# Oldest of four PSUM banks for the small products of attention, and a new order at both ends of it

## Chip, cores and metric

One core of one Trainium2 chip runs the whole program. The metric is device time in microseconds (us), the median over runs of the kernel. PE is TensorE, PEld its weight loads, DVE VectorE, ACT ScalarE, POOL GpSimd, SP SyncE, whose queue issues nearly all DMAs.

## The reference, cut to what matters

```python
scores = scale * q @ k^T                       # 4 batches, 12 heads, 448 x 448, head size 64
scores = einsum('bhij,hg->bgij', scores, w_pre)    # heads are mixed
attn   = softmax(scores)
attn   = einsum('bhij,hg->bgij', attn, w_post)     # heads are mixed again
x      = attn @ v                              # as 1792 tokens x 768
h      = x @ w_in                              # 768 x 2048
x      = (h - tanh(h)) @ w_out                 # 2048 x 768
# then a soft mixture of 8 experts with 4 slots each (phi, w1, w2), output 1792 x 768
```

## The kernel before

Attention (`talking_heads`) cuts each batch's 448 queries into four chunks (120, 120, 120, 88), 16 chunks in all. A chunk is cut into slots of up to 10 queries times 12 heads = 120 rows; there are 180 slots. A slot is the unit of the steady loop: `regroup` (DMA D<-S, issued four slots ahead), `premix` (PE pm, DVE row maximum mx), `expo` (ACT e), `guard`, `recip`, `norm` (POOL and DVE, giving wk), and three slots later `postmix` (PE tm, ACT aT).

Beside these, the loop carries work that prepares or ends whole chunks:

- heads: the scores of a chunk (`scores4`, three calls of two head pairs each), six matmuls sc for each pair and two PSUM banks; ACT copies them to S, the two copies of the odd pair in the slot of the call and those of the even pair in the next slot. S has two buffers, so the copies of chunk m wait until the D<-S of chunk m-2 have read theirs.
- jobs: `k_pair` (transposes kx of the next batch's k, read by ACT as khi and by DVE as klo), `q_half` (transposes qx, read by ACT and DVE as qT), `values` (32 matmuls vx, read by DVE as xs; the third group of a chunk also stores xs to xd). The DVE read of a job stands in the next slot, behind that slot's reciprocal.

The order is written by hand. `plan` puts each piece into a slot before the loop is emitted. Heads stand at fixed slots; `calm` puts q and value jobs into the slot of a window with the least planned PE load. Each engine and the SP queue run in program order.

The PSUM tiles of attention go round eight banks. Two are the premix's (tag p), two the postmix's (t), two have the tag x and two the tag q. Before, kx, vx, qx (from chunk 1 on) and the odd pairs' sc share the two x banks; the even pairs' sc and the first chunk's qx have the two q banks. The q banks' pool closes four slots before the end, when the second part (`moe_and_slots`) starts beside attention's last slots: it splits x and w_in into high and low parts (`split_x`, `split_w`), runs its first two products (hp) and their gates between the last slots, and enters its own loop over 64 products (`step`) when attention has ended (`box["go"]`). Weights go round a ring of three units: `load_w(t)` fills one, `split_w(t)` splits it (ACT, then DVE or POOL), `save_w(t)` stores the split.

From the second part's loop the program goes on to the experts, whose weights are loaded into buffers as the loop frees them.

Of the kernel before, what the change touches and what calls it, by code (L numbers as in the profile page):

```python
# [9 lines left out]
FP32 = mybir.dt.float32  # L10
F32R = mybir.dt.float32r
ACTF = mybir.ActivationFunctionType
# [6 lines left out]
NR = 4  # L19
# [21 lines left out]
def bits(ap):  # L41
    return ap.bitcast(FP32)
# [104 lines left out]
def talking_heads(tc, ident, q, k, v, w_pre, w_post, xd, box, follow):  # L147
# [7 lines left out]
    DB = 5  # L155
    T_LAG = 3
    WARM = 10

    late_stack = ExitStack()
    early_stack = ExitStack()  # L160
# [36 lines left out]
    def kron(name, w, scale, inner_g):  # L197
# [15 lines left out]
            out=m, in_=m, pattern=neg, compare_op=ALU.is_ge, fill=0.0, base=NH - 1, channel_multiplier=-1)  # L213
        return m

    def k_pair(b, p):
        x = ps.tile([128, NR, JP], FP32, tag="x", name="kx", bufs=2)
        src = nat_k.pop((b, p))
        for r in range(NR):
            if b:  # L220
                nc.tensor.transpose(
                    out=x[:, r, :], in_=src[:, r].rearrange("p e d -> p (e d)"), identity=ident[:JP, :JP])
            else:
                for e in range(2):
                    nc.tensor.matmul(
                        x[64 * e:64 * e + 64, r, :], lhsT=src[:, e, r, :], rhs=ident[:JP, :JP], start=True, stop=True)
        x = x.rearrange("p r j -> p (r j)")
        hi = er.tile([128, SEQ], F32R, tag=f"khi{p}", name="khi", bufs=1)
        lo = er.tile([128, SEQ], F32R, tag=f"klo{p}", name="klo", bufs=1)
        nc.scalar.activation(out=hi, in_=x, func=ACTF.Copy)  # L230
        kT[b, p] = hi, lo

        def rest():
            nc.vector.tensor_tensor(out=lo, in0=x, in1=bits(hi), op=ALU.subtract)  # L234

        return rest

    def q_half(n, hf):
        ni = chunks[n][2]
        if hf == 0:  # L240
            qT[n] = er.tile([128, 2, NP, CHUNK], F32R, tag="qT", name="qT")
        t = qT[n][:, :, 3 * hf:3 * hf + 3, :ni]
        x = ps.tile([128, 3, CHUNK], FP32, tag="x", name="qx", bufs=2) if n else psq.tile(
            [128, 3, CHUNK], FP32, tag="q", name="qx")
        for i in range(3):
            p = 3 * hf + i
            nc.tensor.transpose(out=x[:, i, :ni], in_=nat_q[n][:ni, 2 * p:2 * p + 2, :], identity=ident[:ni, :ni])  # L247
        nc.scalar.activation(out=t[:, 0], in_=x[:, :, :ni], func=ACTF.Copy)

        def rest():  # L250
            nc.vector.tensor_tensor(out=t[:, 1], in0=x[:, :, :ni], in1=bits(t[:, 0]), op=ALU.subtract)  # L251

        return rest

    def scores(n, p, on_dve=False):
        b, i0, ni, _ = chunks[n]
        if n not in S_t:
            S_t[n] = er.tile([CHUNK, NH, SEQ], FP32, tag="S", name="S")
        if p % 2:
            xs = [ps.tile([CHUNK, SEQ], FP32, tag="x" if n else "p", name="sc", bufs=2) for _ in range(2)]  # L260
        else:
            xs = [psq.tile([CHUNK, SEQ], FP32, tag="q", name="sc") for _ in range(2)]
        hi, lo = kT[b, p]
        for i, (kt, l) in enumerate(((hi, 0), (lo, 0), (hi, 1))):
            for e in range(2):
                s = slice(64 * e, 64 * e + 64)
                nc.tensor.matmul(  # L267
                    xs[e][:ni], lhsT=qT[n][s, l, p, :ni], rhs=kt[s], start=(i == 0), stop=(i == 2))

        def keep(e):  # L270
            dst = S_t[n][:ni, 2 * p + e, :]
            if on_dve and e:
                nc.vector.tensor_copy(out=dst, in_=xs[e][:ni])
            else:
                nc.scalar.activation(out=dst, in_=xs[e][:ni], func=ACTF.Copy)  # L275

        return [lambda: keep(0), lambda: keep(1)]

# [61 lines left out]
    def values(n, g):  # L340
        b, i0, ni, _ = chunks[n]
        a = attn_t[n]
        if g == 0:
            xs_t[n] = lt.tile([128, NP, CHUNK], FP32, tag="xs", name="xs", bufs=1)
        xs = xs_t[n]
        x = ps.tile([128, 2, CHUNK], FP32, tag="x", name="vx", bufs=2)
        for i in range(2):
            for c in range(NR):
                for e in range(2):
                    h = 4 * g + 2 * i + e  # L350
                    nc.tensor.matmul(  # L351
                        x[64 * e:64 * e + 64, i, :ni], lhsT=nat_v[b, h // NP][:, h % NP, c, :], rhs=a[:, c, h, :ni],
                        start=(c == 0), stop=(c == NR - 1))

        def rest():
            nc.vector.tensor_copy(out=xs[:, 2 * g:2 * g + 2, :ni], in_=x[:, :, :ni])
            if g == 2:
                nc.sync.dma_start(out=xd[b][:, :, i0:i0 + ni], in_=xs[:, :, :ni])

        return rest  # L360
# [4 lines left out]
    def plan(kind, s, *a):  # L365
        at.setdefault((kind, s), []).append(a)
# [12 lines left out]
    for m in range(1, NC):  # L379
        w = len(chunks[m - 1][3])  # L380
        w0 = start[m - 1] - D_AHEAD
        for g in range(3):
            s0 = max(-1, w0 + g * w // 3)
            plan("head", s0, m, g)
            if s0 >= 0:
                load["pe"][s0] += 1.6
            for t in (s0, s0 + 1):
                load["act"][max(t, 0)] += 1.08
    for m in range(1, NC):
        if chunks[m][1] + CHUNK >= SEQ and m + 1 < NC:  # L390
            w = len(chunks[m - 1][3])
            w0 = start[m - 1] - D_AHEAD
            free_at = {}
            for p in range(NP):
                t = w0 + p // 2 * w // 3 + 1 + p % 2
                free_at[p] = t
                job(t, k_pair, chunks[m + 1][0], p, act=0.55, dve=0.62, pe=0.5)
                plan("load", max(t - 6, free_at.get(p - 4, 0) + 1), load_k, chunks[m + 1][0], p)
    for m in range(2, NC):
        t0 = start[m - 2]  # L400
        plan("load", max(0, t0 - 8), load_q, m)
        for lo, hi, hf in ((max(2, t0 - D_AHEAD + 1), t0 + 3, 0), (t0 + 4, start[m - 1] - D_AHEAD - 1, 1)):
            job(calm("pe", lo, hi), q_half, m, hf, act=0.47, dve=0.53, pe=0.4)
    for m in range(NC):
# [42 lines left out]
        nc.tensor.matmul(warm, lhsT=ident, rhs=ident, start=True, stop=True)  # L447
    for p in range(NP):
        k_pair(0, p)()
        if p in (0, 2):  # L450
            q_half(0, p // 2)()
        if p == 3:
            load_q(1)
        if p >= 2:
            for f in scores(0, p - 2, True):
                f()
    for p in range(NP - 2, NP):
        for f in scores(0, p, True):
            f()
    for s in range(D_AHEAD):  # L460
        regroup(s)
    q_half(1, 0)()
# [8 lines left out]
    s = 0  # L471
    while s < NS + T_LAG + 2 or jobs or late:
        live = s < NS
        if s + D_AHEAD < NS:
            regroup(s + D_AHEAD)
        for f, *a in at.get(("load", s), []):
            f(*a)
        if live:
            premix(s)
        if 0 <= s - 1 < NS:  # L480
            recip(s - 1)
        if 0 <= s - 1 < NS:
            norm(s - 1)
        for f in late:
            f()
        late = []
        if 0 <= s - T_LAG < NS:
            postmix(s - T_LAG)
        if live:
            expo(s)  # L490
            guard(s)
        for a in at.get(("head", s), []):
            halves += scores4(*a)
        for f in halves[:2]:
            f()
        halves = halves[2:]
        for f, *a in at.get(("dve", s), []):
            f(*a)
        for f, *a in at.get(("act", s), []):
            f(*a)  # L500
        jobs += at.get(("job", s), [])
        room = 2
        while jobs and room > 0:
            f, *a = jobs.pop(0)
            late.append(f(*a))
            room -= 1
        for f in box["setup"][s - 6:s - 5] if s >= 6 else []:
            f()
        if s == NS - D_AHEAD:
            early_stack.close()  # L510
            more = follow()
        if more is not None:
            next(more)
        s += 1
# [8 lines left out]
def moe_and_slots(tc, ident, xd, wi, wo, wo4, wis, consts, w1, w2, out, box):  # L523
# [107 lines left out]
    def load_w(t):  # L631
        if t < NF:
            nc.sync.dma_start(out=unit(t)[:, :, 1], in_=wi[t].rearrange("p (m i) -> p m i", m=2))
        elif t < NST:
            nc.sync.dma_start(out=unit(t), in_=wis[t % NF])
# [230 lines left out]
    def step(t):  # L866
# [4 lines left out]
            hooks.setdefault(c, []).append(lambda: fn(*a))  # L871

        if t + 2 < LAST + 2:
            load_w(t + 2)
        else:
            on(KD // 2, load_half, t + 2, 0)
            on(KD, load_half, t + 2, 1)
# [74 lines left out]
    gate_last(0)  # L952
    save_w(0)
    load_w(3)
    split_w(2, nc.vector)
    save_w(1)
    yield
    gate_act(1)
    gate_first(1)
    gate_last(1)  # L960
    while not box.get("go"):
        yield
    acc_stack = ExitStack()
    acc = acc_stack.enter_context(tc.tile_pool(name="m_acc", bufs=1, space=PSUM, reuse_waits="tile"))
    for tag in ("h2", "q0", "q1", "r0", "r1", "lg"):
# [310 lines left out]
```

## Time and profile before

| | us |
|---|---|
| median of three runs | 990.23 |
| lowest, highest | 986.09, 991.73 |
| the profiled execution: time | 987.97 |
| the profiled execution: span from first to last instruction | 986.3 |
| span: PE busy | 924.7 |
| span: ACT busy, DVE busy | 571.6, 563.0 |

Busy time of an engine is the time in which it has work in hand; matmuls are pipelined, so a busy PE isn't PE at its peak. Idle time before an instruction is put down to what released it. The granted clock of TensorE is 1.00 at 2.4 GHz; 1.2 GHz stands as 0.5, and a window over both has a value between. In the trace's time the slots run from 23.45 us (first pm) to about 506 us (last pm), and the second part's loop starts at 527.39 us.

### The profile page before, as it was taken

Reading aid. Unit: us, or ns where it says so; the run is one execution under the profiler, and the core shown is the slowest. Engines: PE = TensorE matmul, PEld = TensorE weight load, DVE = VectorE, ACT = ScalarE, POOL = GpSimd, SP = SyncE. Lnnn points to the kernel's source line nnn. Section 1 sums busy time; section 2 is a strip of 40 time slices with the busy share of each in tenths; the row PEclk is TensorE's granted clock in tenths of the full one; section 3 lists DMA queues with packets and bytes.
Section 4 is the critical chain, followed back from the end, with each engine's and each line's share of the span. In section 5 each row is a group of like instructions: output and inputs, shape, how many; then the busy total and the mean of one; then the engine's idle time right before and its main releaser. Section 6 shows DMA issues by size and latency. Waiting matters only on the chain.

```text
span 986.3 us, 19398 instructions
## 1 busy us (share of the span) xinstructions
PE 924.7 (94%) x6952; PEld 685.0 (69%) x6952; DVE 563.0 (57%) x1251; ACT 571.6 (58%) x1291; POOL 267.7 (27%) x467
## 2 busy tenths in 40 slices
PE   8899999989999899999997999999999999789975
PEld 6576777767777677777786777778868877535532
DVE  3476566666566565676544566667677766620103
ACT  4677666766677566777664676547647645401013
POOL 1365445544456344565531222000000000000000
PEclk9999999999999899999998999999999999969988
DMA  4888467885678755685347877688455457689998
GB/s 114 229 217 229 159 204 211 226 233 174 185 211 222 215 179 171 190 254 193 136 164 256 312 260 280 252 348 310 161 194 179 145 143 271 263 316 416 422 396 295
DMA packets 139634, 230.22 MB, mean 233 GB/s; under 512 B 58324, under 2 KB 118804, under 8 KB 134932
## 3 DMA queue, kind: packets, MB, share of 16 engines
q1 hardware_dynamic: 136976, 216.40, 67.4%
q10 hardware_dynamic: 2564, 12.60, 3.2%
q8 instruction: 56, 0.92, 0.4%
q14 instruction: 38, 0.31, 0.1%
HBM read 154.25 MB, written 36.18 MB: 193 GB/s over the span
## 4 chain that ended last, share of the span: by engine, by line
PE 72%; DMA 14%; DVE 5%; ACT 5%; issue 2%; SPq 1%; POOL 1%; ACTq 0%; POOLq 0%; DVEq 0%
PE hp L677 19%; PE pm L297 12%; PE tm L333 11%; PE vx L351 7%; PE sc L267 6%; DMA ex<-in_moe_w_dram 5%; PE gt L731 3%; DMA rg<-wis 2%; DMA rg<-wi 2%; PE sp L851 2%; DMA D<-S 2%; PE lgp L775 1%; PE h L1059 1%; ACT e L306 1%; DMA f<-in_moe_w_in_dram 1%
## 5 line engine op out<-in xcount | busy, mean ns | idle before, releaser
L333 PEld LDWEIGHTS tm<-wk,e 120*112 120x112 f32 (+1 forms) x1440 | 176.1, 179 | 71.9 <-issue 59.7
L299 DVE TENSOR_REDUCE mx<-pm 120x1 f32<-120x448 f32 x180 | 111.8, 621 | 138.9 <-PE pm L297 136.9
L297 PE MATMUL pm<-D,wpre 120*120 120x448 f32 x360 | 176.8, 574 | 3.6 <-ACT e L306 2.6
L333 PE MATMUL tm<-wk,e 120*112 120x120 f32 (+1 forms) x1440 | 178.5, 268 | 0.9 <-POOL wk L323 0.9
L336 ACT ACTIVATE aT<-tm 112x480 f32<-112x480 f32 x180 | 105.6, 587 | 121.1 <-PE tm L333 115.8
L323 POOL TENSOR_SCALAR wk<-wpost,rv 120x120 f32<-120x120 f32 x180 | 129.5, 719 | 144.6 <-PE tm L333 112.4
L677 PE MATMUL hp<-xa,rg 128*128 128x448 f32 x576 | 140.7, 384 | 0.0
L677 PE MATMUL hp<-xb,rg 128*128 128x448 f32 x576 | 133.7, 377 | 1.6 <-DMA rg<-wis 1.5
L677 PEld LDWEIGHTS hp<-xb,rg 128*128 128x128 f32 x576 | 103.8, 188 | 24.2 <-issue 14.2
L677 PEld LDWEIGHTS hp<-xa,rg 128*128 128x128 f32 x576 | 103.9, 192 | 19.1 <-issue 11.7
L306 ACT ACTIVATE e<-pm,mx 120x448 f32<-120x448 f32 x180 | 114.1, 634 | 4.4 <-DVE rv L318 2.3
L275 ACT ACTIVATE S<-sc 120x448 f32<-120x448 f32 (+1 forms) x186 | 91.0, 545 | 14.2 <-PE sc L267 6.6
L1070 POOL MEMSET tq<- 128x256 f32 x8 | 2.4, 312 | 337.7 <-PE sp L851 268.0
L351 PE MATMUL vx<-aT,vn 112*64 112x120 f32 (+1 forms) x1536 | 84.5, 263 | 8.0 <-DVE klo L234 5.2
L705 DVE SCALAR_TENSOR_TENSOR qd<-qd,sq 128x448 f32<-128x448 f32 x62 | 38.5, 620 | 81.2 <-ACT mk L700 81.0
L695 ACT ACTIVATE sq<-hp 128x448 f32<-128x448 f32 x62 | 32.8, 528 | 89.6 <-PE hp L677 89.4
L351 PEld LDWEIGHTS vx<-aT,vn 112*64 112x64 f32 x1536 | 74.4, 137 | 14.3 <-PE qx L247 5.0
L267 PE MATMUL sc<-khi,qT 64*120 64x448 f32 (+1 forms) x384 | 75.1, 385 | 6.5 <-DVE qT L251 6.1
L312 POOL TENSOR_SCALAR rv<-ss 120x1 f32<-120x1 f32 x180 | 41.9, 233 | 114.6 <-ACT e L306 105.8
L297 PEld LDWEIGHTS pm<-D,wpre 120*120 120x120 f32 x360 | 52.2, 184 | 26.4 <-ACT e L306 11.7
L67 POOL TENSOR_TENSOR fa<-fa,f 128x384 f32<-128x384 f32 x64 | 65.2, 1019 | 5.1
L267 PEld LDWEIGHTS sc<-khi,qT 64*120 64x120 f32 (+1 forms) x384 | 41.4, 171 | 20.5 <-PE tm L333 5.8
(166 smaller groups left out, 1261.5 us busy)
## 6 DMA issues: line engine op xcount, KB each, us to landing
ex<-in_moe_w_dram SPq DMA_DIRECT2D x28, 1536.0 KB
D<-S SPq DMA_DIRECT2D x172, 210.0 KB
rg<-wis SPq DMA_DIRECT2D x34, 768.0 KB
f<-in_moe_w_in_dram SPq DMA_DIRECT2D x32, 384.0 KB
f<-in_moe_w_out_dram SPq DMA_DIRECT2D x32, 384.0 KB
wis<-rg ACTq DMA_DIRECT2D x16, 768.0 KB
rg<-wis SPq DMA_DIRECT2D x28, 384.0 KB
wi<-fa SPq DMA_DIRECT2D x32, 192.0 KB
```

What stands on the lines that cost most here:

```text
L67: eng.tensor_tensor(out=out, in0=bits(a), in1=bits(p), op=ALU.add)
L267: nc.tensor.matmul(xs[e][:ni], lhsT=qT[n][s, l, p, :ni], rhs=kt[s], start=(i == 0), stop=(i == 2))
L275: nc.scalar.activation(out=dst, in_=xs[e][:ni], func=ACTF.Copy)
L297: nc.tensor.matmul(x[:r], lhsT=wpre[:r, :m, :], rhs=D_t.pop(s)[:r], start=True, stop=True)
L299: nc.vector.tensor_reduce(out=mx[:r], in_=x[:r], op=ALU.max, axis=AX.X, negate=True)
L306: nc.scalar.activation(out=e[:r], in_=pp_t.pop(s)[:r], func=ACTF.Exp, bias=mx_t.pop(s)[:r], accum_out=ss[:r])
L312: nc.gpsimd.tensor_scalar(out=rv[:r], in0=ss_t.pop(s)[:r], scalar1=EPS, scalar2=None, op0=ALU.add)
L323: nc.gpsimd.tensor_scalar(out=wk[:r], in0=wpost[:r], scalar1=ss_t.pop(s)[:r], scalar2=None, op0=ALU.mult)
L333: nc.tensor.matmul(x[:, c, :, :m], lhsT=e[:r, c * JP:(c + 1) * JP], rhs=wk[:r, :, :m], start=True, stop=True)
L336: nc.scalar.activation(out=attn_t[n][:, :, :, c0:c0 + m], in_=x[:, :, :, :m], func=ACTF.Copy)
L351: nc.tensor.matmul(x[64 * e:64 * e + 64, i, :ni], lhsT=nat_v[b, h // NP][:, h % NP, c, :], rhs=a[:, c, h, :ni], start=(c == 0), stop=(c == ...
L677: nc.tensor.matmul(hp, lhsT=r32(w[:, m, hl, cs]), rhs=r32(x_of(b, c, l)), start=(c == 0 and i == 0), stop=(c == KD - 1 and i == 2))
```

## The change

Four things change in attention and at its two ends.

- Small products get their bank from `small_bank`. It notes for each of the four x and q banks the slot in which its last read was emitted and takes for kx (from batch 1 on), qx (from chunk 2 on) and vx the tag whose next bank was read longest ago, x when equal. Scores keep x for the odd and q for the even pair. In the last four slots only x is used.
- `HEAD_LAG = 1` puts heads, and with them k jobs and k loads, one slot later; the planner also charges 1.0 to the PE load of the slot ahead of each head, which moves q and value jobs in the plan.
- At the start, the second half of the first chunk's q is turned after the scores of pair 1 rather than ahead of those of pair 0, and `load_q(2)` is issued ahead of the first four regroups rather than in slot 0's loads.
- At the end, `load_w(4)` is issued with `load_w(3)`, right after `save_w(1)`, rather than at the start of step 2; `split_w(2)` comes after `gate_act(1)` and a further slot; DVE's part of the gates of product 1 (`gate_first(1)`, `gate_last(1)`) comes after attention has ended, rather than ahead of its last value copies.

```diff
+    HEAD_LAG = 1
...
+    ready = {tag: [-9, -9] for tag in "xq"}
+    turn = {"x": 0, "q": 0}
+    now = [-9]
+
+    def small_bank(shape, name, tag=None):
+        if tag is None:
+            tag = min("xq", key=lambda z: ready[z][turn[z]]) if box["both"] else "x"
+        i = turn[tag]
+        turn[tag] = 1 - i
+        ready[tag][i] = 10 ** 6
+        pool = ps if tag == "x" else psq
+
+        def read():
+            ready[tag][i] = now[0]
+
+        return pool.tile(shape, FP32, tag=tag, name=name, bufs=2), read
...
-        x = ps.tile([128, NR, JP], FP32, tag="x", name="kx", bufs=2)
+        x, read = small_bank([128, NR, JP], "kx", None if b else "x")
...
-        x = ps.tile([128, 3, CHUNK], FP32, tag="x", name="qx", bufs=2) if n else psq.tile(
-            [128, 3, CHUNK], FP32, tag="q", name="qx")
+        x, read = small_bank([128, 3, CHUNK], "qx", None if n > 1 else "x" if n else "q")
...
-        if p % 2:
-            xs = [ps.tile([CHUNK, SEQ], FP32, tag="x" if n else "p", name="sc", bufs=2) for _ in range(2)]
+        if p % 2 and not n:
+            xs = [(ps.tile([CHUNK, SEQ], FP32, tag="p", name="sc", bufs=2), lambda: None) for _ in range(2)]
         else:
-            xs = [psq.tile([CHUNK, SEQ], FP32, tag="q", name="sc") for _ in range(2)]
+            xs = [small_bank([CHUNK, SEQ], "sc", "qx"[p % 2]) for _ in range(2)]
...
-        x = ps.tile([128, 2, CHUNK], FP32, tag="x", name="vx", bufs=2)
+        x, read = small_bank([128, 2, CHUNK], "vx")
...
-            s0 = max(-1, w0 + g * w // 3)
+            s0 = w0 + HEAD_LAG + g * w // 3
+            s0 = max(s0, -1)
             plan("head", s0, m, g)
             if s0 >= 0:
                 load["pe"][s0] += 1.6
+            if s0 >= 1:
+                load["pe"][s0 - 1] += 1.0
...
-                t = w0 + p // 2 * w // 3 + 1 + p % 2
+                t = w0 + HEAD_LAG + p // 2 * w // 3 + 1 + p % 2
...
-        plan("load", max(0, t0 - 8), load_q, m)
+        if m > 2:
+            plan("load", max(0, t0 - 8), load_q, m)
...
-        if p in (0, 2):
-            q_half(0, p // 2)()
+        if p == 0:
+            q_half(0, 0)()
         if p == 3:
             load_q(1)
         if p >= 2:
             for f in scores(0, p - 2, True):
                 f()
+        if p == 3:
+            q_half(0, 1)()
     for p in range(NP - 2, NP):
         for f in scores(0, p, True):
             f()
+    load_q(2)
     for s in range(D_AHEAD):
         regroup(s)
...
+        now[0] = s
+        box["both"] = s < NS - D_AHEAD
...
         if t + 2 < LAST + 2:
-            load_w(t + 2)
+            if t > 2:
+                load_w(t + 2)
...
     save_w(0)
     load_w(3)
-    split_w(2, nc.vector)
     save_w(1)
+    load_w(4)
     yield
     gate_act(1)
+    yield
+    split_w(2, nc.vector)
+    while not box.get("go"):
+        yield
     gate_first(1)
     gate_last(1)
-    while not box.get("go"):
-        yield
```

## Rows read from the trace of the kernel before

**Rows 1.** First part of the page: busy us, share of the span, instructions.

```profile
PE 924.7 (94%) x6952; PEld 685.0 (69%) x6952; DVE 563.0 (57%) x1251; ACT 571.6 (58%) x1291; POOL 267.7 (27%) x467
```

**Rows 2.** Windows: busy us (instructions) of each engine, granted clock, DMA share, GB/s.

```profile
30.00:34.00 4.00, 3.92 (x15) 2.76 (x16) 1.12 (x3) 1.66 (x4) 0.59 (x2) 0.67 1.08 253
...
200.00:300.00 100.00, 94.21 (x818) 72.08 (x818) 64.33 (x162) 68.99 (x173) 47.50 (x85) 1.00 0.68 200
...
324.00:336.00 12.00, 9.57 (x47) 6.89 (x44) 4.82 (x13) 5.88 (x15) 3.28 (x7) 0.72 0.85 227
...
400.00:500.00 100.00, 99.91 (x876) 75.93 (x875) 65.00 (x169) 70.14 (x174) 53.84 (x98) 1.00 0.63 201
...
520.00:530.00 10.00, 7.19 (x106) 6.40 (x106) 5.82 (x12) 3.04 (x5) 1.81 (x1) 0.83 0.66 232
...
540.00:550.00 10.00, 10.00 (x54) 8.85 (x53) 6.25 (x12) 7.07 (x14) 2.62 (x2) 0.83 0.50 171
600.00:800.00 200.00, 198.52 (x1117) 156.28 (x1112) 139.31 (x258) 118.08 (x232) 1.84 (x1) 1.00 0.64 227
```

**Rows 3.** Waits of PE, whole span: us in total, times, longest us.

```profile
PE sc L267 <- DVE qT L251: 6.1, 11, 0.9
...
PE vx L351 <- DVE klo L234: 5.2, 6, 1.1
PE kx L221 <- ACT S L275: 3.8, 2, 2.4
...
PE vx L351 <- DVE xs L356: 2.8, 1, 2.8
...
PE qx L247 <- DMA qn<-in_q_dram: 2.5, 1, 2.5
PE wt L744 <- ACT tq L734: 2.3, 1, 2.3
```

**Rows 4.** Waits of PE between 40 and 500 us.

```profile
PE sc L267 <- DVE qT L251: 4.4, 9, 0.5
```

**Rows 5.** Timeline near 81 us: start, us, engine, work [idle before <- what ended it].

```profile
80.68 0.62 DVE L234 TENSOR_TENSOR klo<-kx,khi 128x448 fp32r<-128x448 f32 x1 [0.23 <-ACT khi L230]
...
81.46 1.86 PE L351 MATMUL vx<-aT,vn 112*64 112x120 f32 x32 [1.13 <-DVE klo L234]
```

**Rows 6.** Timeline near 328 us.

```profile
328.25 0.97 ACT L275 ACTIVATE S<-sc 88x448 f32<-88x448 f32 x2 [3.76 <-DMA wi<-fa]
...
328.85 1.01 PE L221 MATMUL kx<-ident,kn 112*128 112x112 f32 x4 [2.43 <-ACT S L275]
```

**Rows 7.** Timeline of PE, two neighbouring slots without other work.

```profile
408.31 0.93 PE L297 MATMUL pm<-D,wpre 120*120 120x448 f32 x2
...
409.89 0.92 PE L297 MATMUL pm<-D,wpre 120*120 120x448 f32 x2
```

**Rows 8.** Timeline of the first 45 us: head of attention.

```profile
11.72 0.46 PE L267 MATMUL sc<-khi,qT 64*120 64x448 f32 x1 [0.89 <-DVE qT L251]
...
20.39 4.27 SPq L291 DMA_DIRECT2D D<-S  x5
...
24.76 0.46 SPq L194 DMA_DIRECT2D qn<-in_q_dram  x1
...
30.08 0.50 PE L247 MATMUL qx<-ident,qn 120*128 120x120 f32 x3 [2.53 <-DMA qn<-in_q_dram]
```

**Rows 9.** Timeline from 498 to 550 us: end of attention and start of the second part.

```profile
521.28 0.94 DVE L645 TENSOR_TENSOR rg<-rg 128x768 fp32r<-128x768 f32 x1
...
521.80 0.66 ACT L700 ACTIVATE quad<-quad,tlimit 128x448 f32<-128x448 f32 x1
...
525.15 0.57 DVE L356 COPY xs<-vx 128x176 f32<-128x176 f32 x2
...
530.66 10.35 SPq L633 DMA_DIRECT2D rg<-wi  x3
...
536.97 0.84 ACT L644 ACTIVATE rg<-rg 128x768 fp32r<-128x768 f32 x1 [2.88 <-DMA rg<-wi]
```

More of the change, by code (lines that the diff above doesn't have):

```diff
@@ L234, in rest @@
             nc.vector.tensor_tensor(out=lo, in0=x, in1=bits(hi), op=ALU.subtract)
+            read()
         return rest
@@ L251, in rest @@
             nc.vector.tensor_tensor(out=t[:, 1], in0=x[:, :, :ni], in1=bits(t[:, 0]), op=ALU.subtract)
+            read()
         return rest
@@ L267, in scores @@
                 nc.tensor.matmul(
-                    xs[e][:ni], lhsT=qT[n][s, l, p, :ni], rhs=kt[s], start=(i == 0), stop=(i == 2))
+                    xs[e][0][:ni], lhsT=qT[n][s, l, p, :ni], rhs=kt[s], start=(i == 0), stop=(i == 2))
         def keep(e):
@@ L272, in keep @@
             if on_dve and e:
-                nc.vector.tensor_copy(out=dst, in_=xs[e][:ni])
+                nc.vector.tensor_copy(out=dst, in_=xs[e][0][:ni])
             else:
-                nc.scalar.activation(out=dst, in_=xs[e][:ni], func=ACTF.Copy)
+                nc.scalar.activation(out=dst, in_=xs[e][0][:ni], func=ACTF.Copy)
+            xs[e][1]()
         return [lambda: keep(0), lambda: keep(1)]
@@ L356, in rest @@
             nc.vector.tensor_copy(out=xs[:, 2 * g:2 * g + 2, :ni], in_=x[:, :, :ni])
+            read()
             if g == 2:
```

## The prediction

> **What bounds the kernel now.** I read the page's first part, then windows by stage, then the waits of PE, then the timeline at each longer wait. PE is busy 94% of the span, ACT and DVE 58% and 57% [rows 1]: where no stage says otherwise, PE's own stream sets the pace. The windows say where it doesn't. From 400 to 500 us PE has work in hand for 99.91 of 100 us; from 200 to 300 us, with the same kind of slots, for 94.21; from 600 to 800 us for 198.5 of 200 [rows 2]. So in attention's middle some 5% is lost to waits, late in attention nothing, and in the second part's loop nothing: time won ahead of 560 us comes out at the end, for nothing there waits for anything but PE's order and buffers that PE frees.
>
> The waits name the losses. Those that bear on this change: scores for DVE's read of qT, 6.1 us in 11 waits; values for klo, 5.2 in 6; k turns for ACT's S copies, 3.8 in 2; a value group for xs, 2.8; a q turn for its load, 2.5; wt for ACT, 2.3 [rows 3]. That is 22.7 us. To these comes the clock: it is granted at half for a part of the windows at 30, 324, 520 and 540 us, which show 0.67, 0.72, 0.83 and 0.83 [rows 2]. A window of T us at clock c has lost T(1-c): 1.3, 3.4, 1.7 and 1.7 us. Ahead of the fall near 328 us PE had waited 2.43 us [rows 6]; waits of up to 1.1 us, such as the one at 81 us [rows 5], occur in stretches that hold 1.00.
>
> **The change part by part.** The profiled execution took 987.97 us, 2.3 under the median of 990.23; the sum is made against the first and the 2.3 added at the end.
>
> *A, values behind klo.* In the plan before, the last slot ahead of some heads holds a q turn and a value group, and the slot ahead of that a k turn. With two x banks the third of these needs the bank of the first, whose DVE read is emitted only in the same slot: at 81.46 values wait 1.13 us for the klo begun at 80.68 [rows 5]. By the planner's arithmetic the new order (slot 22: k and q; slot 23: k and values; 25: head) gives these four products the banks x, x, q, q: four banks, each read at least one slot earlier. All six waits go: -5.2 us [rows 3]. Ends: 0, if another read is late instead, and -5.2.
>
> *B, scores behind qT.* Of the 11 waits nine lie in the steady part, 4.4 us, 0.5 the longest [rows 3, 4]. They come where a q or value job shares the slot ahead of a head, since the odd pair needs both x banks. The charge of 1.0 moves those jobs away from that slot: -4.4. Against it: jobs may now sit in q banks, and the even pair needs both of those. There are 45 calls of heads; a wait of 0.5 at each would cost 22 us. That is the bad end. Since the even pair runs behind the odd one and k turns fall one and two slots behind a head, I take 8 such waits, +4.0, and the good end is 0.
>
> *C, heads one slot later.* The S copies near 328 us waited 3.76 us on ACT for a transfer, and the k turn behind them 2.43 [rows 6]. By the code this is the D<-S of the chunk two before, issued at the start of the slot ahead. A slot without other work lasts 409.89 - 408.31 = 1.58 us [rows 7], so 2.43 shrinks to 0.85, and the other k wait (3.8 - 2.4 = 1.4 [rows 3]) goes: -2.9. A wait of 0.85 is like those that left the clock at 1.00, so the 3.4 of the window at 324 us goes too: together -6.3. Ends: 0, if the transfer is simply later, and -7.2. Later heads also finish S later: their D<-S are issued four slots ahead, over 6 us even by 1.58 each, so a delay of a slot on SP is covered; if the cover were gone, each chunk's first premix would wait up to one slot, 15 x 1.58 = 24 us. Everything queued behind such a D<-S on SP (conversion loads and stores, k loads) moves by as much.
>
> *D, the start.* The second score matmul waits 0.89 us for DVE's read of the second q turn [rows 8]; turned later, that read holds up pair 2 for a part of it. -0.6, between 0 and -0.9. `load_q(2)` is issued at 24.76, behind five D<-S from 20.39 on, and the turn at 30.08 waits 2.53 for it [rows 8]. Issued ahead of them it needs only the first q's turns, which end long before 20.39, on an SP queue with nothing else to do; the D<-S lose nothing: -2.5 (ends 0, -2.5). Of the 1.3 us of slow clock behind that gap I take -1.0 (ends 0, -1.3). Sum -4.1.
>
> *E, the end.* DVE copies xs at 525.15, behind both products' gates, and the last value group waits 2.8 us for it [rows 9, 3]. After the change the second gates stand behind the copies, but `split_w(2)` still ahead, and its ACT part now behind `gate_act(1)`, whose last instruction ends at 521.80 + 0.66. Adding ACT's 0.84 and DVE's 0.94 [rows 9] gives 524.2 for the copies: -0.9 only, and 1.9 us of gap stays, so I leave that clock loss. The moved gates are hidden by product 2; the next to need them is the turn in step 3. `load_w(4)` is the first of three issues from 530.66 on; ACT waits 2.88 us for it at 536.97, its later work for `turn_g` is late, and PE's wt waits 2.3 [rows 9, 3]. Issued right after `save_w(1)`, some 9 us earlier, it lands in time: -2.3, and the 1.7 of slow clock behind it. SP waits there for that save's landing, with only attention's last xd store behind it, which has the last value group to wait for anyway. Sum -4.9; ends -0.9 and, with all of the gap and both clock losses, -8.5.
>
> Sum: -5.2 - 4.4 + 4.0 - 6.3 - 4.1 - 4.9 = -20.9, so 967.1 against the execution's own time and **969** against the median.
>
> A rule that speaks against A and B: the Trainium skill (TensorE: Matmul & The Clock Gate, section HAM oscillation — how this bites in real kernels) tells of a kernel whose order left no long gaps, and to which double-buffered PSUM then gave nothing, 126.6 to 125.5 us. By it A and B count 0, and the sum would be 967.1 + 9.6 = 976.7. The trace has 9.6 us of waits on readers of banks [rows 3, 4], which speak for the larger gain; no run here has yet shown which holds.
>
> **The rivals.**
> 1. *Half is absorbed.* ACT runs 69 of 100 us in the steady stretch [rows 2] and catches up while PE waits. With the gaps gone, e and aT come nearer to PE's need. For: in two neighbouring bare slots there is 1.58 us for what ACT does in one slot. Against: from 400 to 500 us PE runs without gaps and ACT still has 30 us idle [rows 2]. Half of A to C (15.9) is 8.0: 975.1, or 977.
> 2. *More banks give nothing,* the waits move to the next reader in DVE's order. A and B are 0: 976.7, or 979. Against: DVE runs 64 of 100 us there.
> 3. *Slower: even pairs wait for q banks.* Small products now hold q banks, and the even pair finds one unread. Without B the gains are 5.2 + 6.3 + 4.1 + 4.9 = 20.5 us; over 45 calls this decides from 0.46 us a call on. At the 1.1 us of the longest klo wait [rows 3] it costs 49.5: 987.97 - 20.5 + 49.5 = 1017, or 1019. For: waits of 0.5 do occur on the x side. Against: only nine of them.
> 4. *No change in the middle.* Loads and D<-S come a slot later and DMA is at 0.85 near 328 us [rows 2]: what A to C give goes into waits for transfers. Left are D and E with the 4.0 against them: 983.0, or 985, the edge of no change.
>
> **How the numbers follow.** Forecast 0.52; rival 1 0.22; rival 2 0.10; rival 4 0.10; rival 3 0.06. Half a per cent of 990.23, about what a measurement of this kernel can tell from no change, is 5 us: faster means under 985.3. Forecast and rivals 1 and 2 are faster, and rival 4 stands on the edge, so I count nearly all of it as no change and a little of rival 3 too: faster 0.83, same 0.12, slower 0.05. The forecast's own range is 960 (all good ends of A to E without the 4.0: 987.97 - 5.2 - 4.4 - 7.2 - 4.7 - 8.5 = 958.0, or 960) to 976, where rival 1 begins; to leave out no more than 2 in 10 it reaches to rivals 1 and 2 and most of the way to 4: 960 to 984.
>
> **What would show it.** A: no wait of vx for klo. B: waits of sc for qT only in the first 25 us. C: k turns wait under 1 us, and no slow clock between 40 and 500 us. D: the q turn near 27 us starts without a wait for its load. E: load_w(4) issued ahead of the last xd store, no wait of wt for tq, the last value group some 1.9 us behind its predecessor. Together, the last pm about 16 to 20 us earlier than 506. Wrong if sc waits for vx's or kx's reads, if pm waits for e or D more than now, or if the last pm is early and the end isn't.

## The result, and the profile after

The changed kernel takes 962.34 us, the median of four runs (956.96 to 964.61); the kernel before, on the same chip, 990.98 (986.09 to 992.05). The ratio is 0.971, 95% interval 0.966 to 0.977: 28.6 us faster, outside what a measurement can mistake for no change. The profiled execution took 964.55 us, 23.4 less than the 987.97 of the one before.

The first part of the page after, in the columns of [rows 1]:

```profile
PE 916.1 (95%) x6952; PEld 678.8 (71%) x6952; DVE 566.3 (59%) x1251; ACT 571.1 (59%) x1291; POOL 265.8 (28%) x467
```

PE carries out the same 6952 matmuls, yet is busy for 8.6 us less. The span fell by 23.5 us (986.3 to 962.8), so idle time gave 14.9 of it and busy time the rest. The waits of PE after, whole span, in the columns of [rows 3]:

```profile
PE pm L317 <- ACT e L326: 4.1, 8, 0.7
...
PE pm L317 <- DMA D<-S: 2.5, 2, 2.2
PE kx L239 <- ACT S L294: 2.4, 1, 2.4
...
PE vx L371 <- DVE xs L376: 1.8, 1, 1.8
...
PE wt L774 <- DMA ex<-wo: 1.1, 1, 1.1
...
PE wt L774 <- ACT ex L778: 0.9, 1, 0.9
...
PE sc L286 <- DVE qT L269: 0.8, 1, 0.8
```

Values no longer wait for klo (5.2 us before), no turn waits for its load of q (2.5), wt no longer waits for tq (2.3), and scores wait once, for 0.8 us, where they waited eleven times for 6.1. One k turn still waits 2.43 us for the S copies. Two kinds of wait have grown: pm for ACT's e (2.6 us in five before, 4.1 in eight now) and pm for D (0.3 in one before, 2.5 in two now). And wt now waits 2.0 us in all for a load (ex) and for ACT.

To see the middle by itself I cut both traces at the same work: from the first pm of slot 12 to the first pm of slot 179, the last slot. First all work, then sc alone, before:

```profile
52.27:505.46 453.19, 436.60 (x3717) 331.94 (x3717) 287.70 (x730) 311.86 (x774) 224.55 (x406) 0.99 0.69 203
52.27:505.46 453.19, 65.46 (x492) 43.36 (x492) 0.00 (x0) 79.95 (x164) 0.99 0.69 203
```

The same two windows after:

```profile
49.03:484.27 435.24, 428.84 (x3719) 327.12 (x3718) 289.55 (x731) 312.00 (x776) 222.26 (x404) 1.00 0.72 211
49.03:484.27 435.24, 60.47 (x492) 39.69 (x492) 0.00 (x0) 80.01 (x165) 1.00 0.72 211
```

The stretch lost 453.19 - 435.24 = 17.95 us. PE's idle time went from 453.19 - 436.60 = 16.6 us to 6.4, a gain of 10.2; its busy time fell by 7.8. Of that, 5.0 are the same 492 score matmuls, and 1.7 are clock: 6.83 us at half speed in the middle before, 3.41 after. The start gave 52.27 - 49.03 = 3.2 us. The start of the seventh product (hp), 556.25 before and 530.76 after, is 25.5 us earlier, so the end of attention gave 25.5 - 3.2 - 17.95 = 4.3; by the end of the span 2.1 us of all this are lost again.

Why would the same matmuls be busy for less time? One call of scores before, PE's timeline:

```profile
85.57 0.73 PE L267 MATMUL sc<-khi,qT 64*88 64x448 f32 x2 [0.49 <-DVE qT L251]
85.88 0.61 PE L267 MATMUL sc<-klo,qT 64*88 64x448 f32 x2
...
87.24 1.01 PE L297 MATMUL pm<-D,wpre 120*120 120x448 f32 x2
```

and the same call after:

```profile
81.91 0.43 PE L286 MATMUL sc<-khi,qT 64*88 64x448 f32 x2
82.18 0.36 PE L286 MATMUL sc<-klo,qT 64*88 64x448 f32 x2
...
83.30 1.01 PE L317 MATMUL pm<-D,wpre 120*120 120x448 f32 x2
```

A pair is two heads, each in 64 of the 128 rows of the array and in a bank of its own. After, the two of a row start together: x2 in 0.43 us. Before, the first started when a q job's read (qT) of its bank had ended, and the second 0.31 us later, when DVE's xs copy, the read of a value group that held the other x bank, had ended (85.34 + 0.40); so the two ran side by side only in part (x2 in 0.73 us), and the call took 87.24 - 85.57 = 1.67 us rather than 83.30 - 81.91 = 1.39. The list of waits shows the 0.49 ahead of the call; the 0.28 inside it counts as busy.

Windows after, columns of [rows 2], around the clock:

```profile
30.00:34.00 4.00, 3.88 (x24) 2.73 (x25) 2.13 (x7) 3.59 (x11) 2.13 (x5) 1.00 0.92 238
...
194.00:202.00 8.00, 5.57 (x47) 4.57 (x46) 3.51 (x8) 4.76 (x12) 2.41 (x5) 0.79 0.96 254
316.00:324.00 8.00, 8.00 (x76) 6.37 (x76) 6.43 (x18) 6.27 (x16) 4.43 (x9) 1.00 0.94 246
36.00:46.00 10.00, 7.80 (x42) 5.70 (x41) 4.52 (x12) 6.52 (x17) 4.77 (x12) 0.83 0.89 233
...
505.00:515.00 10.00, 8.93 (x52) 7.84 (x51) 7.26 (x13) 4.54 (x8) 2.81 (x2) 1.00 1.01 334
515.00:525.00 10.00, 9.08 (x56) 7.93 (x55) 4.87 (x10) 7.57 (x15) 3.10 (x2) 1.00 0.73 228
```

The half clock at 31, 328, 526 and 540 us (6.83 us of it at 328, 3.41 at each of the others) is gone. In its place stand two falls of 3.41 us, at 41.2 and at 198.2 us. (Both kernels also run parts of their experts at half clock, from 861 us before and 833 after.) The second follows the k turn's wait. ACT and PE there, after:

```profile
195.24 0.54 ACT L46 ACTIVATE fa<-f 128x384 f32<-128x384 f32 x1 [2.71 <-DMA f<-in_moe_w_out_dram]
...
196.75 0.96 ACT L294 ACTIVATE S<-sc 88x448 f32<-88x448 f32 x2
...
197.33 0.60 PE L239 MATMUL kx<-ident,kn 112*128 112x112 f32 x4 [2.43 <-ACT S L294]
```

It has the same form as [rows 6], but not the same cause. Before, the S copies themselves waited for a transfer; here they waited for nothing, and stand in ACT's queue behind a conversion of w_out (f to fa) that waits 2.71 us for its load.

The start, after:

```profile
12.79 0.33 SPq L195 DMA_DIRECT2D qn<-in_q_dram  x1
19.11 6.04 SPq L311 DMA_DIRECT2D D<-S  x7
...
29.42 3.78 SPq L90 DMA_DIRECT2D f<-in_moe_w_in_dram  x1
33.30 5.14 SPq L311 DMA_DIRECT2D D<-S  x4
...
40.78 0.67 PE L317 MATMUL pm<-D,wpre 120*120 120x448 f32 x1 [2.19 <-DMA D<-S]
```

`load_q(2)` goes out at 12.79 rather than 24.76 [rows 8], and its turn waits for nothing. At 40.78 a premix waits 2.19 us for its D, whose D<-S stood on SP behind a conversion load (f) that took 3.78 us to issue. And the end of attention, after:

```profile
499.74 2.48 SPq L663 DMA_DIRECT2D rg<-wi  x2
502.91 0.58 DVE L376 COPY xs<-vx 128x176 f32<-128x176 f32 x2
503.30 1.44 PE L371 MATMUL vx<-aT,vn 112*64 112x88 f32 x32 [1.77 <-DVE xs L376]
505.15 0.57 SPq L379 DMA_DIRECT2D xd<-xs  x1
510.20 0.83 ACT L674 ACTIVATE rg<-rg 128x768 fp32r<-128x768 f32 x1
```

`load_w(4)` is one of the two issues from 499.74 on, ahead of the last xd store; ACT's split at 510.20 finds its weights there. The last value group waits 1.77 us instead of 2.8.

### The profile page after: what moved, and what is told of

The parts are those of the page before. It is cut to its first block, busy times and chain, and to the rows that moved or that the text cites. A ratio compares the mean times of both kernels' runs of the same rounds, so it can differ in the third digit from the quotient of the medians.

```text
span 962.8 us, 19390 instructions
## 1 busy us (share of the span) xinstructions
PE 916.1 (95%) x6952; PEld 678.8 (71%) x6952; DVE 566.3 (59%) x1251; ACT 571.1 (59%) x1291; POOL 265.8 (28%) x467
## 4 chain that ended last, share of the span: by engine, by line
PE 81%; DMA 9%; ACT 4%; DVE 3%; issue 2%; POOL 0%; SPq 0%; ACTq 0%; POOLq 0%; DVEq 0%
PE hp L707 21%; PE pm L317 14%; PE tm L353 13%; PE vx L371 7%; PE sc L286 6%; PE gt L761 3%; PE h L1092 2%; PE sp L881 2%; PE so L1131 2%; DMA ex<-in_moe_w_dram 2%; DMA f<-in_moe_w_in_dram 2%; DMA rg<-wi 2%; DMA rg<-wis 2%; PE lgp L805 1%; PE tz L1110 1%
## 5 line engine op out<-in xcount | busy, mean ns | idle before, releaser
L707 PE MATMUL hp<-xa,rg 128*128 128x448 f32 x576 | 138.5, 380 | 0.6 <-POOL rg L675 0.6
L286 PE MATMUL sc<-khi,qT 64*120 64x448 f32 (+1 forms) x384 | 69.1, 388 | 0.8 <-DVE qT L269 0.8
L332 POOL TENSOR_SCALAR rv<-ss 120x1 f32<-120x1 f32 x180 | 41.2, 229 | 103.6 <-ACT e L326 92.3
L46 ACT ACTIVATE fa<-f 128x384 f32<-128x384 f32 x64 | 35.8, 559 | 18.8 <-DMA f<-in_moe_w_in_dram 15.3
```

Source lines behind the costliest of these rows:

```text
L286: nc.tensor.matmul(xs[e][0][:ni], lhsT=qT[n][s, l, p, :ni], rhs=kt[s], start=(i == 0), stop=(i == 2))
L332: nc.gpsimd.tensor_scalar(out=rv[:r], in0=ss_t.pop(s)[:r], scalar1=EPS, scalar2=None, op0=ALU.add)
L707: nc.tensor.matmul(hp, lhsT=r32(w[:, m, hl, cs]), rhs=r32(x_of(b, c, l)), start=(c == 0 and i == 0), stop=(c == KD - 1 and i == 2))
```

## The experiments

The theory is the prediction's: each edit removes its own waits, and what was under-counted is the scores, whose waits also hide in busy time. The rivals are that ACT or the next bank reader takes the gains (rivals 1 and 2), that even pairs pay for them (3), and that only the ends count (4). All kernels compute the whole reference. Each ratio is to the kernel before on the same chip. The times named in the first four expectations count from the 990 us of the first chip, so it is the differences that are to be compared.

| kernel | us | before there | ratio (95%) |
|---|---|---|---|
| bank_alone | 971.64 | 984.39 | 0.987 (0.984 to 0.990) |
| lag_alone | 976.35 | 984.39 | 0.992 (0.989 to 0.994) |
| bank_and_lag | 967.92 | 984.39 | 0.985 (0.981 to 0.988) |
| ends_alone | 980.35 | 984.39 | 0.996 (0.994 to 0.998) |
| after_again (the change, unaltered) | 961.50 | 986.07 | 0.975 (0.972 to 0.979) |
| no_charge | 968.47 | 986.07 | 0.982 (0.979 to 0.986) |
| late_v | 962.26 | 986.07 | 0.976 (0.973 to 0.980) |
| cv4 | 957.09 | 986.07 | 0.969 (0.965 to 0.973) |
| no_bank | 970.53 | 983.75 | 0.985 (0.982 to 0.988) |
| no_lag | 968.09 | 983.75 | 0.984 (0.981 to 0.987) |
| cv4_before | 984.80 | 983.75 | 1.001 (0.999 to 1.003) |
| cv4_late_v | 953.15 | 983.75 | 0.969 (0.966 to 0.972) |

And the same cut through the middle (first pm of slot 12 to that of slot 179), read from one window of each trace as above, us:

```
                before  after  after_again  bank_alone  lag_alone  bank_and_lag  no_charge  no_bank  no_lag  cv4
stretch         453.19  435.24   437.66       441.18     445.01      439.62       443.05    445.65   441.01  427.04
PE idle in it    16.59    6.40     7.40         8.57      14.46        8.74         6.94     13.78     9.19    0.49
sc busy in it    65.46   60.47    60.49        63.95      60.47       60.47        70.48     60.47    61.82   60.53
```

after and after_again are the same kernel: two traces of it differ by 2.4 us here. The scores fill 41 calls of this stretch. In the kernel before, 15 of them have a pair whose two matmuls start apart; bank_alone has 12, no_charge 28, no_lag 3, and the others none.

**One part of the change alone.** bank_alone has `small_bank` and none of the rest (against the changed kernel, its part for the middle; the start and the end are put back as well):

```diff
-    HEAD_LAG = 1
+    HEAD_LAG = 0
...
-            if s0 >= 1:
-                load["pe"][s0 - 1] += 1.0
```

> The kernel before with the choice among four banks alone (old plan, old ends). Theory: in attention's middle the 20 us came from products that found their bank unread, so the choice removes the waits of vx for klo (5.2 us) and lets a q or value job ahead of a head sit in a q bank, so that part of the 11 us lost around the scores goes too: 10 us less, about 980. Rival, the plan did it: jobs still share the slot ahead of heads, scores still need all four banks, only the 5 us of vx go: about 985. Rival, banks give nothing: 990.

Measured: -12.75 us, where 10 were expected. The wait of vx for klo is gone. The scores' waits are 3.2 us in 5 over the whole span, so the banks by themselves free part of them; the k turns' waits for S grew from 3.8 to 5.1. Its waits between 40 and 490 us:

```profile
PE kx L239 <- ACT S L294: 5.1, 3, 2.5
PE pm L317 <- ACT e L326: 2.0, 5, 0.6
PE sc L286 <- DVE qT L269: 1.5, 3, 0.5
```

lag_alone has `HEAD_LAG` and the charge, keeps all small products on x, and has the old start and end (not shown):

```diff
-            tag = min("xq", key=lambda z: ready[z][turn[z]]) if box["both"] else "x"
+            tag = "x"
```

> The kernel before with heads, k jobs and k loads one slot later and the planner's charge, small products still in the x banks. Theory: the 11 us around the scores go by the charge, and of the S copies' waits 3 us; the waits of vx for klo stay, since the plan now puts k, q, k, values into two neighbouring slots with two banks: about 980, with 5 us of vx waits still in the profile or more. Rival, banks did it all: about 988, with waits of sc for qT as before.

Measured: -8.0 us. Scores wait only in the first 25 us and are busy 60.47 us in the middle, as in the full change, but the k turns now wait 10.7 us:

```profile
PE kx L239 <- PE tm L353: 5.6, 7, 1.0
PE kx L239 <- issue: 5.1, 2, 3.9
```

Each of these nine k turns starts 0.10 us after DVE's read of the klo before it has ended, whatever the list names.

bank_and_lag has both and the old ends.

> Both of these, old ends. Theory: the two add up to the middle's 20 us: about 970, last premix some 18 to 20 us earlier than before. If the start's 3 us were only won because the middle had room, or the reverse, it differs from 962 by more than the 6 us that the ends should hold.

Measured: -16.5 us, less than 12.75 + 8.0, and the last premix only 15.5 us earlier (489.95): the two do not add up as expected. Both take away waits of the scores, which can be taken away only once (of 4.4 us, 1.5 are left in bank_alone and none in lag_alone); what else they share is not shown. The profiled execution took 976.97 us, the slowest of its six runs.

ends_alone has the start and the end and nothing in the middle.

> The reordered loads, turn and gates at both ends alone. Theory: 4 to 5 us won by slot 8, of which 2 are given back by slot 12 to a wait for a transfer (the DMA queue is full there), and 3 to 4 us won between the last premix and the fourth product: 983 to 985. Rival: the start's gain stays whole without the other changes: 981.

Measured: -4.0 us, less than the 5 to 7 that the theory's parts sum to; in the trace 4.0 us are won by slot 8, 2.8 are left by slot 12, and 2.2 more are won from slot 179 to the seventh product. The middle's waits are where they were:

```profile
PE vx L371 <- DVE klo L252: 6.0, 6, 1.1
PE sc L286 <- DVE qT L269: 4.4, 9, 0.5
```

A by-product: the k turn near 328 us waits here as before, 2.35 us, and the window around it keeps the full clock.

```profile
326.33 0.60 PE L239 MATMUL kx<-ident,kn 112*128 112x112 f32 x4 [2.35 <-ACT S L294]
...
320.00:340.00 20.00, 16.04 (x131) 12.09 (x130) 10.68 (x29) 11.44 (x29) 7.54 (x15) 1.00 0.88 249
```

**One part taken out.** no_charge drops the 1.0 that the planner charges ahead of a head:

```diff
-            if s0 >= 1:
-                load["pe"][s0 - 1] += 1.0
```

> The changed kernel without the planner's charge for the slot ahead of a head; heads stay one slot late. Theory: the charge only chooses slots for jobs that the four banks already serve, so the time moves by less than 3 us, up if at all, with some waits of sc for qT back. Rival: the charge is what freed the scores: waits of 4 to 9 us back, 5 us or more slower than the changed kernel.

Measured: 968.47 against 961.50, 7.0 us lost: not the theory's 3, but what the rival said. Scores wait for qT again, eight times for 7.2 us between 24 and 490 us. One of them, PE and DVE:

```profile
56.28 0.39 PE L265 MATMUL qx<-ident,qn 88*128 88x88 f32 x3
...
58.30 0.46 PE L286 MATMUL sc<-khi,qT 64*120 64x448 f32 x1
...
59.58 0.41 DVE L269 TENSOR_TENSOR qT<-qx,qT 128x264 fp32r<-128x264 f32 x1
...
60.14 0.43 PE L286 MATMUL sc<-khi,qT 64*120 64x448 f32 x1 [1.38 <-DVE qT L269]
```

A q job stands in the slot ahead of the head once more, and its bank is one of the x banks, the one read longest ago. The call begins with the odd pair, which needs both x banks: its first matmul runs at 58.30, its second waits until DVE has read that job's bank. In bank_alone and no_lag too, each wait of scores that is listed for the middle is at the first or second matmul of a call, the odd pair's.

The list doesn't show all of it. Of the 28 calls whose pairs start apart here, seven have a wait in the middle's list. In 15 the odd pair's second matmul starts 0.4 us late while the first still runs. In the other six it is the even pair, as rival 3 has it, that finds a q bank unread. One of these, DVE, PE and its weight loads:

```profile
83.64 0.40 DVE L376 COPY xs<-vx 128x240 f32<-128x240 f32 x1
83.78 0.81 PE L286 MATMUL sc<-khi,qT 64*88 64x448 f32 x4
84.15 0.15 PEld L286 LDWEIGHTS sc<-khi,qT 64*88 64x88 f32 x1 [0.17 <-PE sc L286]
```

The xs copy ends at 84.03, and the last of the four matmuls, the even pair's second, starts at 84.18; after the change the same four are done in 0.58 us. It costs such a call 0.23 us (1.69 of busy time instead of 1.46), and nothing of it stands in the list of waits. bank_alone has six such calls as well.

PE's idle time in the middle hardly differs from the full change's (6.94 and 6.40); the scores' busy time does, by 10.0 us. The sum of idle time would have missed this loss: nearly all of the 6.94 are waits of scores, 6.8 us, and the waits of k turns and of pm for e that make up the 6.40 are gone.

no_bank is the full change with the small products on x, by the edit of lag_alone.

> The changed kernel with its small products held in the x banks as before; plan, lag, charge and ends stay. Theory: the new plan puts k, q, k and values into two neighbouring slots, so with two banks the waits of kx and vx for DVE's reads are back, 5 to 10 us: about 969. Rival, the plan alone does it: within 2 us of the changed kernel.

Measured: 0.985 against the change's 0.975 on another chip, some 9 us. The k turns wait again. The list names PE's tm, but that had been done; the timeline shows what came last, DVE's read of klo, 75.33 + 0.62 = 75.95:

```profile
75.33 0.62 DVE L252 TENSOR_TENSOR klo<-kx,khi 128x448 fp32r<-128x448 f32 x1 [0.36 <-ACT khi L248]
...
76.05 0.57 PE L239 MATMUL kx<-ident,kn 112*128 112x112 f32 x4 [1.00 <-PE tm L353]
```

no_lag is the full change with `HEAD_LAG = 0`; the charge stays.

> The changed kernel with heads, k jobs and k loads at their old slots, the charge kept. Theory: the lag itself is worth little, since what held the S copies near 200 us in the changed kernel was a late conversion load and not their own transfer: within 3 us of the changed kernel. Rival, as the prediction had it: S copies wait for D<-S again, k turns behind them, and the clock falls: 5 us slower, about 967.

Measured: 0.984 against 0.975 on another chip, some 8.5 us lost, where I had come to expect little. The transfer of [rows 6] is back ahead of the S copies, and the k turn behind them:

```profile
317.59 0.97 ACT L294 ACTIVATE S<-sc 88x448 f32<-88x448 f32 x2 [3.85 <-DMA wi<-fa]
...
318.18 1.01 PE L239 MATMUL kx<-ident,kn 112*128 112x112 f32 x4 [2.53 <-ACT S L294]
```

So the extra slot does what step C says: it gives the D<-S of the chunk two before the time to read S. It isn't the whole of the loss: with the heads the plan moves too, and three calls of scores wait for qT again, 2.5 us in all.

**What still waits after the change.** after_again repeats it, late_v tries the early wait of pm for D, and cv4 the wait of the k turn:

```diff
 late_v
-        plan("load", s0 + 2, load_v, b, 0)
-        plan("load", s0 + T_LAG + (10 if b else 6), load_v, b, 1)
+        plan("load", s0 + (2 if b else 9), load_v, b, 0)
+        plan("load", s0 + T_LAG + (10 if b else 11), load_v, b, 1)
 cv4
-        self.bufs = 3
+        self.bufs = 4
-    done = [0, 0, 0]
+    done = [0] * cv.bufs
-        plan("load", max(a - 4, done[i] + 2), cv.load, j)
+        plan("load", max(a - 7, done[i] + 2), cv.load, j)
```

> The changed kernel once more, beside the three others on one chip. If the parts add up as they did alone (banks and plan together 16 us, ends 4), it stands 20 us under the kernel before here; the first measurement had 28. Theory: the larger one was partly chance of the chip and the executions, and it comes out between 20 and 24.

Measured: 961.50, 24.6 us under the kernel before there, just above the expected 20 to 24; its interval overlaps that of the first measurement (28.6 us). The k turn waits 3.0 us, at 196.56, and the clock falls there too, for 6.8 us.

> The changed kernel with the two loads of the first batch's v seven and five slots later. Theory: the wait of a premix for D near 40 us (2.2 us, with 1.7 us of slow clock behind it) comes of a DMA queue that is full between 25 and 40 us, and goes when the v load leaves it: 3 to 4 us less than the changed kernel. Rival: the queue is full of what else is due, and the wait moves or stays: no change.

Measured: 962.26, no difference. The first v loads aren't what makes D late, at least not by an amount that shows.

> The changed kernel with a fourth buffer for the weight conversion and its loads up to three slots earlier. Theory: what is left of the k turns' wait (2.4 us with slow clock behind it near 200 us) is not the S copies' own transfer but ACT held by a conversion whose load lands late; with the buffer that wait of ACT shrinks, and 3 to 5 us go. Rival: the S copies wait for their own transfer, as the prediction had it: the waits of kx stay at 2 us or more, no change in time.

Measured: 957.09, 4.4 us less than after_again. The intervals of the two ratios overlap a little, but all six runs lie under the lowest of after_again's (952.58 to 958.52, 958.78 to 967.63). Clearest is the trace: between 24 and 490 us no k turn waits, and ACT no longer waits for any conversion load between 40 and 470 us, where it had waited 16.2 + 4.5 us in after_again. Waits of PE in cv4 between 40 and 470 us, whole list:

```profile
PE pm L317 <- DMA D<-S: 3.1, 1, 3.1
PE pm L317 <- ACT e L326: 0.2, 1, 0.2
```

The 3.1 us lie at 42.75, ahead of the middle, in which PE is idle for 0.49 us of 427.04.

cv4_before puts the fourth buffer and the earlier loads into the kernel before.

> The kernel before with the fourth conversion buffer and earlier conversion loads alone. Theory: ACT waited 19 us for conversion loads there too, but PE's waits were others (banks), so this gives less than on the changed kernel, 0 to 3 us. Rival: it gives the same 4 to 5 us, the two are independent.

Measured: 1.001, nothing. Between 40 and 470 us ACT no longer waits for a conversion load (18.9 us before), yet the waits of vx for klo (6.0), sc for qT (4.4) and kx for S (4.4) are all there: they weren't ACT's wait for conversions.

cv4_late_v joins the two on top of the change.

> The changed kernel with the fourth conversion buffer and the first batch's v loads later. With the fourth buffer more conversion loads are issued in the first 40 us, and a premix waits 3.1 us for D. Theory: the later v loads make room there, 2 to 3 us less than with the buffer alone, about 954. Rival: no change against the buffer alone.

Measured: 953.15, the same ratio as cv4, so late_v adds nothing here either that the intervals can tell. Between 24 and 475 us PE is out of work for 1.7 us:

```profile
24.00:475.00 451.00, 449.30 (x3864) 341.79 (x3865) 305.18 (x768) 332.33 (x823) 233.73 (x431) 1.00 0.74 217
```

## Why the prediction was right, and where it was not

The time, 962.3, lies in the range (960 to 984) and 7 us under the forecast. Between the two profiled executions the gain was 23.4 us, 2.5 more than the sum of 20.9. The rest of the 7 us is not a step of the sum: I added 2.3 because the execution before lay 2.3 us under its median, and the one after lay 2.2 over its own.

- **A, right.** -5.2 was forecast, and the 5.2 us are gone. bank_alone shows that the banks do it by themselves. lag_alone and no_bank show that the new plan doesn't: without the banks the same late read of klo catches the next k turn instead of the values.
- **B, the cause right, the price wrong; this is the step that failed.** I counted -4.4 for the waits that the list shows, and +4.0 for new ones of the even pairs, -0.4 in all. Measured in the middle: -4.4 of idle time, -5.0 of busy time of sc, and no new wait: -9.4. The +4.0 was 8 calls of 0.5 us; in the change no call's pairs start apart. Even pairs do wait for q banks in bank_alone and no_charge, in six calls each, at 0.23 us a call. That the charge frees the pairs, as B says, no_charge shows: without it q jobs are back in the slot ahead of a head. The -5.0 I could have had from the trace before: a matmul of a pair that starts late while the other runs doesn't show as idle, but it does show in the time that one call takes.
- **C, the cause right, the size half or less.** -6.3 was forecast (2.9 of waits, 3.4 of clock); measured -1.4 of k waits and -1.7 of clock (6.83 us at half speed before, 3.41 after), -3.1. In after_again, the same kernel, the k wait is 3.04 us and the clock is at half for 6.83 us again, so that little of C is left there. "K turns wait under 1 us, and no slow clock between 40 and 500" did not come true. no_lag shows that the transfer was the cause of [rows 6] and that the slot cures it; cv4 shows that what is left is another one, ACT's queue held by a conversion whose load is late. And ends_alone shows that the clock's part was never as sure as I put it: the same wait, at full clock.
- **D, right, but partly given back.** -4.1 was forecast. The first pm of slot 8 is 5.3 us earlier (42.15 to 36.85), that of slot 12 3.2: between them lie the wait for D at 40.78 and the clock behind it. after_again has such a wait too, 1.98 us, and no fall of the clock there, and is 5.5 us earlier at slot 12. That the D<-S would lose nothing is not borne out, but nor is it shown that the start's order brings this wait: bank_and_lag, with the old start, has 1.2 us of such waits.
- **E, the sum close, by luck.** -4.9 was forecast, -4.3 measured up to the seventh product. The last group's gap is 1.77 us (1.9 forecast), and `load_w(4)` left ahead of the last xd store. But of the 2.3 us that wt waited for tq, 2.0 came back as its waits for a load (ex) and for ACT, which I had not counted; all of E's idle time is only 1.3 us less (6.4 and 5.1). What made up for it is the clock: both falls are gone (6.83 us at half speed, 3.4 lost), of which I had counted one. And that isn't sure: in no_charge, no_bank, no_lag and cv4 the last group waits the same 1.77 us, and half clock follows for 3.41 us.
- **The whole.** The last pm stands at 484.27, 21.2 us earlier (16 to 20 forecast). The terms of the middle sum to -5.2 - 9.4 - 3.1 + 0.7 (pm for e and fa, 3.1 before, 3.8 after) = -17.0 of the 17.95; the last 0.9 I can't place. The second trace of the changed kernel has 15.5 in place of 17.95. The 2.1 us lost again behind the seventh product aren't shown to be the change's: that stretch takes 430.0 us before, 432.1 after and 427.8 in after_again. One of the signs of being wrong came, in small: pm waits more than before for e (4.1 us for 2.6) and for D (2.5 for 0.3).

**The rivals.** Rival 1 (half absorbed by ACT) would have left 8.0 us from the middle; it gave 18, and 15.5 in after_again. Of its mechanism there is a trace: pm's waits for e grew by 1.5 us over the span. The one longer time that ACT holds PE comes of its queue order, not of its load. Rival 2 falls with bank_alone, -12.75 us for banks alone. (Its 976.7 still held the 4.0 of B; with A and B at nothing the sum is 987.97 - 6.3 - 4.1 - 4.9 = 972.7.) The rule of the Trainium skill behind it (TensorE: Matmul & The Clock Gate, section HAM oscillation — how this bites in real kernels), that double-buffered PSUM gave nothing to a kernel without long gaps, doesn't carry over: here 9.6 us of gaps were waits on the reads of banks, and the measurement decides. Rival 4 falls with ends_alone, -4.0 of some 25. Rival 3's mechanism is real but small: six calls at 0.23 us in bank_alone and in no_charge, where it needed 0.46 at each of 45; most of what came back in no_charge is the odd pair's, and even there the kernel is faster than before (0.982).

**Open.** The ends alone are worth 4 us; on top of bank_and_lag it is some 9 (0.985 to 0.975, two chips), but with intervals of about 0.004 on each of the three ratios that difference isn't shown by the times. In the traces, from slot 179 to the seventh product, the old end takes 50.8 us before and 51.1, 51.2 and 51.8 in bank_alone, lag_alone and bank_and_lag; the new one takes 46.5 after and 47.0 in after_again, but 48.5 in ends_alone. So it is the new end that does better behind the new middle; why was not tested.

Nor does one price hold for each part of the middle. Taken out of the whole, the banks are worth 9 us, the charge 7 and the extra slot 8.5, more together than the 16 to 18 of the middle. The banks gain 12.0 us of the stretch without the other two. The charge and the extra slot need each other: with four banks the stretch is 441.2 us with neither (bank_alone), 441.0 with the charge alone (no_lag), 443.0 with the extra slot alone (no_charge), and 435.2 and 437.7 with both. Each number is from one trace, and two traces of one kernel differ by 2.4.

## What to carry to other kernels

Where two matmuls share the array, price a late bank by the busy time of the group per call as well as by the idle time ahead of it: half of this loss stood as busy. Where buffers are chosen by how long ago they were read, look at the plan too: the oldest bank can be the one that is needed next, and here it took the charge to keep jobs away from it (no call of scores starts a pair apart after the change, 28 of 41 without the charge). And when a wait has survived its cure, look at what stands ahead of the awaited instruction in its engine's queue: the cause may be a load that neither side uses, as the conversion loads were here.

## What the runs showed of the hardware that I had not expected

- A wait of PE of some 2.4 us may or may not come with half clock: 2.43 us at 328 before, 6.83 us of half clock; 2.43 at 197 after, 3.41 us; 2.35 at 326 in ends_alone, none. Shorter ones differ too: 1.77 us ahead of the last value group comes with 3.41 us in no_charge and none in after. What decides was not found.
- A pair's heads that start apart make the same matmuls dearer in busy time: 65.46 (before), 60.47 (after) and 70.48 us (no_charge) for the same 492 score matmuls in the middle.
- One DMA took SP 3.78 us to issue (the f load at 29.42 after, 3.81 in after_again; the two f loads just ahead of it took 0.5), while the DMA engines were busy for 0.92 of the time (30 to 34 us). The premix whose D<-S stood behind it waited 2.19 us; that the one caused the other was not tested.
